# Pooled attention and a two-layer network: k of six batches loaded in blocks of 32 columns and transposed by VectorE, the second batch's q in rows and by TensorE

## The chip, the cores and the metric

The kernel runs on one core of one Trainium2 chip. The metric is the device time of one execution in microseconds (us). A profiled execution has a span, from its first instruction to its last, and an execution time that is a little longer.

## The reference, cut to what matters

q, k and v have shape (8, 8, 576, 64): 8 batches, 8 heads, 576 positions, 64 values. k and v are averaged over groups of eight rows, so each head has 72 keys.

```python
k_p = k.reshape(B, H, Sp, pool, D).mean(axis=3)      # Sp = 72, pool = 8
v_p = v.reshape(B, H, Sp, pool, D).mean(axis=3)
scores = scale * q @ k_p.T ; scores -= max(scores)
attn = exp(scores) / (sum(exp(scores)) + 1e-9)
x = (attn @ v_p).transpose(0, 2, 1, 3).reshape(4608, 512)
h = x @ w_in                                         # 512 x 2048
out = maximum(0.01 * h, h) @ w_out                   # 2048 x 512
```

All is float32. q and k are drawn eight times larger than the usual tenth of a normal draw.

## The kernel before, in words

**The network** takes most of the time. The 4608 rows of x are worked in nine chunks of 512. For each of 16 slices f of the inner size, `m1` (L745) multiplies (ph, four pieces of the model size, L754 to L756), applies the leaky step on ScalarE (L759) and splits the result into a high and a low part (gh L762, gl L763); `m2` (L767) multiplies back into four accumulators (acc, L778 to L780). Each product is three matmuls, high by high, low by high and high by low, in a reduced-precision type; the weights are split in the same way once, early, by `convert` (L169): L184, L185 and L194 on ScalarE, L186, L187, L190 and L195 on VectorE. The chunks go through in "runs" (L738): the first eight slices of chunk 0, all of chunk 1, the other eight of chunk 0, then chunks 2 to 8.

**The attention** of a batch is cut into tiles of 128 positions (and one of 64), the tiles into pieces (`PIECES`, L60), and its steps are put in between the slices of the network. The order of TensorE is written out by hand: for batch 0 in `FIRST`, for batch 1 and 2 by `line_up` (L644), from batch 3 on (`VIA`) by `line_up_via` (L701). The other engines and the queues of DMAs follow the order that the scheduler works out from this. The steps are:

- `load_k` (L265): k of a batch is read as two tiles of 128 partitions (k0 and k1, L241: 64 pooled keys of two heads on each) and one of 64 partitions for the last 8 keys (krem, L251). `pooled` (L226) adds eight rows in three steps (L229, L229, L235), by VectorE for batch 0 and by GpSimd after that. k's last sum is written twice, side by side (copies=2). v is loaded in the same way (L289, with vrem, L259, for its last keys).
- `place_k` (L335): TensorE transposes the sums (pk, four, and pkr for the last keys), ScalarE (L339, L346) and VectorE (L340, L347) scale them into kT, in which the heads of a pair stand in separate halves.
- `load_q` (L316): for batch 0 a tile of q is one DMA in rows; for the others it is 16 DMAs (L332), each of one block of 32 columns of every other row group, in pieces of 128 bytes. `q_unit` (L375) turns a tile: for batch 0 by four TensorE transposes (pq, L385) and a ScalarE copy (L387), for the others by one VectorE transpose of 32 by 32 blocks (L381).
- `s_unit` (L403): scores of four heads (pss, L410), the maximum (red, L418), four exponentials with their sums (e, L420).
- `norm_unit` (L428) divides (L431, L432 on VectorE, `at` L434 and L438 on GpSimd) and TensorE transposes `at` (pp, L500). From batch 3 on `norm_via` (L447; L450, L451, `at` L454 and L460) writes `at` to memory (`rows`, L466) and `fetch_via` (L469) reads it back in 32-column blocks (`blocks`, four DMAs for each, L475), which VectorE transposes (L480).
- `p_unit` (L493) splits that (L502, L503 on ScalarE, L506, L510 on VectorE) and `av_unit` (L514) multiplies by v (pa, L525 to L528). Its result is x of the network.

All loads, and `rows`, `blocks` and the stores of the output, are issued from SyncE's one queue (SPq), in order. The `raw` tiles of a batch's k0, k1, krem, v0, v1 and vrem take turns in two buffers, so krem can be issued only once the sums of k0 are done, and v0 once those of k1 are done. q has two buffers, `at` and `blocks` share three, the tiles with tag `o` (output, weight conversion, transposed `blocks`) three. A batch's k and v are loaded about one run ahead. PSUM gives batch 0 eight banks for its steps; every later batch has two (`bank`, L207).

Of the kernel before, what the change touches and what calls it, by code (L numbers as in the profile page):

```python
# [10 lines left out]
F32 = mybir.dt.float32  # L11
# [4 lines left out]
ALU = mybir.AluOpType  # L16
# [8 lines left out]
def tile_pooled_attention_ffn(  # L25
# [9 lines left out]
    nc = tc.nc  # L35

    P = 128
    B, H, S, D = q.shape
    POOL = 8
    SP = S // POOL  # L40
    MAIN = 64
    REM = SP - MAIN
    DM, DFF = moe_w_in.shape
    NK = DM // P
# [27 lines left out]
    KSCALE = 1.0 / (POOL * 8.0)  # L72
# [3 lines left out]
    one = ctx.enter_context(tc.tile_pool(name="one", bufs=1))  # L76
    two = ctx.enter_context(tc.tile_pool(name="two", bufs=2))
    five = ctx.enter_context(tc.tile_pool(name="outs", bufs=3))
# [15 lines left out]
        out=copies, in_=ident.rearrange("p (h c j) -> p c h j", h=4, c=4), axis=AX.XY, op=ALU.add  # L94
# [6 lines left out]
        out=heads, in_=ident.rearrange("p (h x) -> p h x", h=4), axis=AX.X, op=ALU.add  # L101
# [6 lines left out]
    for g in range(2):  # L108
        r = slice(32 * g, 32 * g + 32)
# [6 lines left out]
    kT = const.tile([P, NK, 2, SP], F32, name="kT")  # L116
# [29 lines left out]
    def spare(f, i, shape, dtype, name):  # L146

        return wts.tile(shape, dtype, tag=f"w{i}_{f}", name=name)
# [58 lines left out]
    def bank(b, name):  # L207
        nonlocal turn
        pool, tag = banks[turn % len(banks)] if b == 0 else banks[0]
        turn += 1  # L210
        return pool.tile([P, NK, P], F32, tag=tag, name=name)
# [8 lines left out]
    def raw_tile(b, nm):  # L220
        shape = [P, 2, POOL * D]
        if (b, nm) in RAW:
            return spare(*RAW[b, nm], shape, F32, f"{nm}raw{b}")
        return two.tile(shape, F32, tag="raw", name=f"{nm}raw{b}")

    def pooled(eng, dst, raw, n, copies=1):  # L226

        for w in (256, 128):
            eng.tensor_tensor(  # L229
                raw[:n, :, 0:w], raw[:n, :, 0:w], raw[:n, :, w : 2 * w], op=ALU.add  # L230
            )
        a, b = raw[:n, :, 0:64], raw[:n, :, 64:128]
        if copies > 1:
            a, b = (x.unsqueeze(2).broadcast_to(dst.shape) for x in (a, b))
        eng.tensor_tensor(dst, a, b, op=ALU.add)  # L235

    def load_main(b, src, g, nm):

        raw = raw_tile(b, f"{nm}{g}")
        for i in range(2):  # L240
            nc.sync.dma_start(  # L241
                raw[64 * i : 64 * i + 64, :, :],
                src[b, 4 * g + i : 4 * g + 4 : 2, : MAIN * POOL, :].rearrange(
                    "p (s a) d -> s p (a d)", a=POOL
                ),
            )
        return raw

    def load_k_rem(b):
        raw = raw_tile(b, "krem")  # L250
        nc.sync.dma_start(  # L251
            raw[:64, 0, :],
            k[b, :, MAIN * POOL :, :].rearrange("h (s a) d -> h s (a d)", a=POOL),
        )
        return raw

    def load_v_rem(b):
# [4 lines left out]
        )  # L262
        return raw

    def load_k(b):  # L265
        sums = one.tile([P, NK, 2, D], F32, tag="ksum", name=f"ksum{b}")
        rem = one.tile([64, 1, 2, D], F32, tag="kremsum", name=f"kremsum{b}")
        eng = nc.vector if b == 0 else nc.gpsimd
        raws = []

        def start():
            raws.extend(load_main(b, k, g, "k") for g in range(2))
            raws.append(load_k_rem(b))

        def finish():
            if b > 1:
                raws.append(load_main(b, k, 0, "k"))
            pooled(eng, sums[:, 0:2], raws[0], P, 2)
            if b > 1:
                raws.append(load_main(b, k, 1, "k"))  # L280
            pooled(eng, sums[:, 2:4], raws[1], P, 2)
            if b > 1:
                raws.append(load_k_rem(b))
            pooled(eng, rem, raws[2][:, 0:1, :], 64, 2)
            return sums, rem

        return start, finish
# [28 lines left out]
    def load_q(b, t):  # L316
        s0, n = tiles[b][t]
        if b == 0:
            qr = one.tile([P, H, D], F32, tag=f"xh1_{t}" if t < NK else "xl1_0", name=f"q{b}_{t}")
        else:  # L320
            qr = two.tile([P, H, D], F32, tag="q", name=f"q{b}_{t}")
        if b == 0:
            nc.sync.dma_start(qr[:n], q[b, :, s0 : s0 + n, :].rearrange("h s d -> s h d"))
            return qr

        blocks = qr.rearrange("a h d -> a (h d)").rearrange("a (p g d) -> a p g d", p=NK, d=32)
        src = q[b, :, s0 : s0 + n, :].rearrange("(p i) (g s) (c d) -> i c s p g d", i=2, s=32, c=2)
        for i in range(2):
            for c in range(2):
                r = 32 * (2 * i + c)  # L330
                for p in range(NK):
                    nc.sync.dma_start(blocks[r : r + 32, p, : n // 32, :], src[i, c, :, p])  # L332
        return qr

    def place_k(b, sums, rem):  # L335
        pk = bank(b, f"pk{b}")
        for p in range(NK):
            nc.tensor.transpose(pk[:, p, :], sums[:, p, :, :].rearrange("s i d -> s (i d)"), ident)
        nc.scalar.mul(kT[0:64, :, 0, 0:MAIN], pk[0:64, :, 0:64], KSCALE)  # L339
        nc.vector.tensor_scalar_mul(kT[64:128, :, 1, 0:MAIN], pk[64:128, :, 64:128], KSCALE)  # L340
        pr = bank(b, f"pkr{b}")
        nc.tensor.transpose(
            pr[:, 0, 0:64], rem.rearrange("s o i d -> s (o i d)"), ident[:64, :64]
        )
        prv = pr[:, 0, 0:64].rearrange("d (p i j) -> d p i j", p=NK, i=2)
        nc.scalar.mul(kT[0:64, :, 0, MAIN:], prv[0:64, :, 0, :], KSCALE)  # L346
        nc.vector.tensor_scalar_mul(kT[64:128, :, 1, MAIN:], prv[64:128, :, 1, :], KSCALE)  # L347
# [26 lines left out]

    def q_unit(b, t, qr):  # L375
        n = tiles[b][t][1]
        if b > 0:

            qT = two.tile([P, NK, P], F32, tag="qT", name=f"qT{b}_{t}")
            blocks = qr.rearrange("a h d -> a (h d)").rearrange("a (p s) -> a p s", p=NK)  # L380
            nc.vector.transpose(qT[:, :, :n], blocks[:, :, :n])  # L381
            return qT
        pq = bank(b, f"pq{b}_{t}")
        for p in range(NK):
            nc.tensor.transpose(pq[:, p, :n], qr[:n, 2 * p : 2 * p + 2, :], ident[:n, :n])  # L385
        qT = two.tile([P, NK, P], F32, tag="qT", name=f"qT{b}_{t}")
        nc.scalar.copy(qT[:, :, :n], pq[:, :, :n])  # L387
        return qT
# [183 lines left out]
    def attention(b):  # L572
# [5 lines left out]
        def loads():  # L578
            (start_k, st["k"]), (start_v, st["v"]) = load_k(b), load_v(b)
            start_k()  # L580
            q_of[b, 0] = load_q(b, 0)
            q_of[b, 1] = load_q(b, 1)
            start_v()
            for t in range(2, 5):
                q_of[b, t] = load_q(b, t)

        def loads1():
            (start_k, st["k"]), (start_v, st["v"]) = load_k(b), load_v(b)
            start_k()
            start_v()  # L590

        def lk():
            st["ks"] = load_k(b)[1]() if b > 1 else st["k"]()
# [4 lines left out]
        def ku():  # L598
            place_k(b, *st["ks"])
# [4 lines left out]
        def qu(t):  # L604
            def f():
                st["qT", t] = q_unit(b, t, q_of[b, t])
                after = every.index((b, t)) + 2
                if after < len(every) and every[after] not in q_of:
                    q_of[every[after]] = load_q(*every[after])
            return f  # L610
# [245 lines left out]
    for b in range(2, B):  # L856
        for j, piece in enumerate(PIECES[b]):
            c = 2 + (2 * TAIL + S * (b - 2) + piece[0][0]) // CH
# [89 lines left out]
```

## Time and profile before

| | |
|---|---|
| time, median of three runs | 984.65 us (981.51 to 985.26) |
| the profiled execution's own time | 983.37 us |
| its span | 981.6 us |
| mean granted TensorE clock | 0.974 |
| TensorE busy | 922.0 us |
| VectorE, ScalarE, GpSimd busy | 410.2, 414.5, 185.4 us |

A row of the profile names a group of instructions, or one, by its line in the kernel, its engine and the names of what it writes and reads. PE is TensorE, DVE VectorE, ACT ScalarE, POOL GpSimd, and SPq the queue of DMAs that SyncE issues. In a timeline a row begins with its start and its length in us, and the bracket at its end tells how long the engine was idle before it and what ended that. In a table by stretches a row holds the span, then busy time and instructions of PE, PE's weight loads, DVE, ACT and POOL, then the granted clock (1.00 is full speed), the busy share of the 16 DMA engines and GB/s.

### The profile page before, as it was taken

What the parts mean: (1) busy time and instruction counts of PE and PEld (TensorE: products, weight loads), DVE (VectorE), ACT (ScalarE), POOL (GpSimd) and SP (SyncE); (2) the same over time, 40 slices, a digit from 0 to 9 for tenths busy, and PEclk for the clock granted to TensorE, in tenths of its full rate; (3) what the DMA queues carried; (4) which work ended last, traced back from release to release, by engine and by line L of the source; (5) the groups of instructions that cost most, each with busy time, mean ns of one, the idle gap of its engine ahead of it and who ended that gap; (6) DMA issues with size and microseconds to landing.
All of it is one profiled execution on the core that took longest, in us unless ns stands there. A gap on an engine that the chain in (4) does not pass through costs nothing. (4 is left out here: it accounts for less than half of the span.)

```text
span 981.6 us, 13210 instructions
## 1 busy us (share of the span) xinstructions
PE 922.0 (94%) x4246; PEld 757.0 (77%) x4246; DVE 410.2 (42%) x987; ACT 414.5 (42%) x1351; POOL 185.4 (19%) x342
## 2 busy tenths in 40 slices
PE   4557989999999998999999999999999999999998
PEld 4446768888887877888888888777878888888886
DVE  5978757513324324334333543354334532321111
ACT  4756766423434333434343444343444433332212
POOL 3610120220106540132112321231111001000000
PEclk8677999999999999999999999999999999999999
DMA  9765332231005432242223332332222110201001
GB/s 249 190 187 158 107 89 67 68 90 46 15 11 145 123 92 50 79 105 61 65 83 87 85 81 79 76 73 65 67 49 63 49 52 25 48 1 44 1 1 43
DMA packets 138469, 75.21 MB, mean 77 GB/s; under 512 B 107552, under 2 KB 121504, under 8 KB 138400
## 3 DMA queue, kind: packets, MB, share of 16 engines
q1 hardware_dynamic: 138400, 74.38, 28.8%
q8 instruction: 33, 0.54, 0.2%
q14 instruction: 36, 0.29, 0.1%
HBM read 54.98 MB, written 19.33 MB: 76 GB/s over the span
## 5 line engine op out<-in xcount | busy, mean ns | idle before, releaser
L754 PE MATMUL ph<-xh,w 128*128 128x512 f32 x576 | 231.2, 401 | 0.0
L778 PE MATMUL acc<-w,gh 128*128 128x512 f32 x576 | 231.0, 401 | 0.0
L756 PE MATMUL ph<-xh,w 128*128 128x512 f32 x576 | 226.6, 393 | 0.0
L755 PE MATMUL ph<-xl,w 128*128 128x512 f32 x576 | 226.6, 393 | 0.0
L779 PE MATMUL acc<-w,gh 128*128 128x512 f32 x576 | 225.8, 392 | 0.0
L780 PE MATMUL acc<-w,gl 128*128 128x512 f32 x576 | 225.7, 392 | 0.0
L763 DVE TENSOR_TENSOR gl<-ph,gh 128x512 fp32r<-128x512 f32 x144 | 98.9, 686 | 242.0 <-ACT gh L762 241.0
L759 ACT ACTIVATE ph<-ph 128x512 f32<-128x512 f32 x144 | 84.1, 584 | 267.2 <-PE ph L756 267.1
L420 ACT ACTIVATE e<-pss,red 128x72 f32<-128x72 f32 (+1 forms) x320 | 98.0, 320 | 92.8 <-DVE red L418 92.3
L756 PEld LDWEIGHTS ph<-xh,w 128*128 128x128 f32 x576 | 109.2, 190 | 23.7
L780 PEld LDWEIGHTS acc<-w,gl 128*128 128x128 f32 x576 | 108.7, 189 | 23.5
L754 PEld LDWEIGHTS ph<-xh,w 128*128 128x128 f32 x576 | 109.0, 189 | 23.1 <-issue 1.6
L778 PEld LDWEIGHTS acc<-w,gh 128*128 128x128 f32 x576 | 108.7, 189 | 22.7 <-issue 1.4
L755 PEld LDWEIGHTS ph<-xl,w 128*128 128x128 f32 x576 | 109.2, 190 | 21.0
L779 PEld LDWEIGHTS acc<-w,gh 128*128 128x128 f32 x576 | 108.8, 189 | 20.7
L454 POOL TENSOR_TENSOR at<-e,red 128x128 f32<-128x128 f32 (+1 forms) x100 | 37.8, 398 | 318.3 <-DVE red L451 216.5
L762 ACT CAST gh<-ph 128x512 fp32r<-128x512 f32 x144 | 84.7, 588 | 3.7
L418 DVE TENSOR_REDUCE red<-pss 128x4 f32<-128x288 f32 (+1 forms) x80 | 36.0, 452 | 82.6 <-PE pss L410 82.5
L420 ACT ACTIVATION_READ_ACCUMULATOR e<-pss,red 128x1 f32 (+1 forms) x320 | 65.7, 205 | 0.0
L502 ACT CAST pT_hi<-pp 128x256 fp32r<-128x256 f32 (+1 forms) x80 | 30.0, 378 | 81.0 <-DVE pp L480 67.3
L410 PEld LDWEIGHTS pss<-kT,qT 128*128 128x128 f32 (+1 forms) x320 | 48.2, 188 | 19.6 <-ACT qT L387 5.0
L410 PE MATMUL pss<-kT,qT 128*128 128x144 f32 (+1 forms) x320 | 55.1, 300 | 8.8 <-ACT qT L387 4.2
(99 smaller groups left out, 818.2 us busy)
## 6 DMA issues: line engine op xcount, KB each, us to landing
out_dram<-o SPq DMA_DIRECT2D x35, 256.0 KB
w_bits<-in_moe_w_in_dram SPq DMA_DIRECT2D x16, 512.0 KB
w_bits<-in_moe_w_out_dram SPq DMA_DIRECT2D x16, 512.0 KB
rows<-at SPq DMA_DIRECT2D x40, 192.0 KB
blocks<-rows SPq DMA_DIRECT2D x160, 48.0 KB
q<-in_q_dram SPq DMA_DIRECT2D x448, 16.0 KB
k0raw<-in_k_dram SPq DMA_DIRECT2D x16, 256.0 KB
k1raw<-in_k_dram SPq DMA_DIRECT2D x16, 256.0 KB
```

The lines of the kernel that those rows point to most:

```text
L410: nc.tensor.matmul(sc[:n, 2 * SP * i : 2 * SP * (i + 1)], qT[:, p, :n], kT[:, p, :, :].rearrange("d i s -> d (i s)"), start=True, stop=True,)
L420: ins = nc.scalar.activation(e[:n, h, :], scv[:n, h, :], AF.Exp, bias=mx[:n, h : h + 1], accum_out=sm[:n, h : h + 1],)
L454: nc.gpsimd.tensor_tensor(at[:n, :, i, :].rearrange("a (h f) j -> a h f j", h=2), e[:n, 2 * i : 2 * i + 2, 0:MAIN].rearrange("a h (f j) -> ...
L754: nc.tensor.matmul(ph, w[:, 0, ks], xh[kk], start=kk == 0, stop=False)
L755: nc.tensor.matmul(ph, w[:, 0, ks], xl[kk], start=False, stop=False)
L756: nc.tensor.matmul(ph, w[:, 1, ks], xh[kk], start=False, stop=kk == NK - 1)
L759: nc.scalar.activation(ph, ph, AF.Prelu, alpha=0.01)
L762: casts.append(nc.scalar.copy(gh, ph))
L763: nc.vector.tensor_tensor(gl, ph, gh.bitcast(F32), op=ALU.subtract)
L778: nc.tensor.matmul(a, gh[:, r], hi, start=first, stop=False)
L779: nc.tensor.matmul(a, gh[:, r], lo, start=False, stop=False)
L780: nc.tensor.matmul(a, gl[:, r], hi, start=False, stop=last)
```

## The change

Two things are changed. For batches 2 to 7, k is read by 8 DMAs into each of the two main tiles and 16 into the tile of the last keys, in pieces of 128 bytes, such that each partition holds one pooled key of one half of a head's 64 columns. GpSimd adds eight rows in three steps (fold) into one tile of sums, not written twice any more. VectorE transposes the sums in blocks of 32 by 32 into a tile kt (tag `o`), and ScalarE and VectorE scale kt into kT. No TensorE transpose of k is left in these batches. For batch 1, a tile of q is read by one DMA in rows and turned by TensorE and ScalarE, as batch 0's is.

```diff
+    def load_k_blocks(b):
+        sums = one.tile([P, NK * SP], F32, tag="ksum", name=f"ksum{b}")
+        main = sums[:, : NK * MAIN].rearrange("a (p k d) -> a p k d", p=NK, k=2)
+        rem = sums[:, NK * MAIN :]
+
+        def fold(raw, out):
+            for w in (4, 2):
+                nc.gpsimd.tensor_tensor(
+                    raw[:, :, 0:w], raw[:, :, 0:w], raw[:, :, w : 2 * w], op=ALU.add
+                )
+            nc.gpsimd.tensor_tensor(out, raw[:, :, 0], raw[:, :, 1], op=ALU.add)
+
+        def finish():
+            for g in range(2):
+                raw = raw_tile(b, f"k{g}")
+                for i in range(2):
+                    for c in range(2):
+                        r = 32 * (2 * i + c)
+                        for p in range(2):
+                            nc.sync.dma_start(
+                                raw[r : r + 32, p, :].rearrange("s (a d) -> s a d", d=32),
+                                k[b, 4 * g + 2 * p + i, : MAIN * POOL, 32 * c : 32 * c + 32].rearrange(
+                                    "(s a) d -> s a d", a=2 * POOL
+                                ),
+                            )
+                fold(...)
+            raw = raw_tile(b, "krem")
+            for i in range(2):
+                for c in range(2):
+                    for p in range(NK):
+                        r = 32 * (2 * i + c) + 8 * p
+                        nc.sync.dma_start(
...
+            fold(raw[:, 0:1, : POOL * 32].rearrange("x o (a d) -> x o a d", d=32), rem.unsqueeze(1))
+            return main, rem
+        return None, finish
+
     def load_k(b):
+        if b > 1:
+            return load_k_blocks(b)
...
     def load_q(b, t):
-        if b == 0:
+        if b < 2:
             nc.sync.dma_start(qr[:n], q[b, :, s0 : s0 + n, :].rearrange("h s d -> s h d"))
             return qr
...
     def place_k(b, sums, rem):
+        if b > 1:
+            t = five.tile([P, NK, SP], F32, tag="o", name=f"kt{b}")
+            nc.vector.transpose(
+                t[:, :, 0:MAIN].rearrange("d p (s k) -> d p k s", k=2), sums
+            )
+            nc.vector.transpose(t[:, :, MAIN:], rem)
+            nc.scalar.mul(kT[0:64, :, 0, :], t[0:64], KSCALE)
+            nc.vector.tensor_scalar_mul(kT[64:128, :, 1, :], t[64:128], KSCALE)
+            return
...
     def q_unit(b, t, qr):
-        if b > 0:
+        if b > 1:
```

**VectorE, between 49 and 62 us.** Before (w_t and w are steps of the weight conversion, qT_0 and qT_1 tiles of batch 1, red_4_0 and red_4_1 the maximum and then the sum of batch 0's last tile; the ISA at L190 is the custom instruction of the conversion):

```order
L190 ISA w_t_534<-w_bits_178,w_t_534 128x1024
L381 STREAM_TRANSPOSE qT_0_771<-q_0_365 128x512
L543 TENSOR_TENSOR xl_3_424<-pa_1_3_561,xh_3_420 128x256
L187 SCALAR_TENSOR_TENSOR w_t_599<-w_bits_180,w_t_599 128x512
L418 TENSOR_REDUCE red_4_0_611<-pss_4_0_607 64x4
L418 TENSOR_REDUCE red_4_1_621<-pss_4_1_617 64x4
L381 STREAM_TRANSPOSE qT_1_838<-q_1_581 128x512
L195 TENSOR_TENSOR w_2_533<-w_t_534,w_2_533 128x512
L190 ISA w_t_599<-w_bits_180,w_t_599 128x1024
L431 TENSOR_SCALAR red_4_0_611<-red_4_0_611 64x4
L432 RECIPROCAL red_4_0_611<-red_4_0_611 64x4
```

Now the same place on VectorE (lines after L265 stand further down in the changed kernel: L605 was L543, L480 was L418, L493 was L431, L494 was L432):

```order
L190 ISA w_t_519<-w_bits_178,w_t_519 128x1024
L605 TENSOR_TENSOR xl_3_409<-pa_1_3_546,xh_3_405 128x256
L187 SCALAR_TENSOR_TENSOR w_t_569<-w_bits_180,w_t_569 128x512
L480 TENSOR_REDUCE red_4_0_581<-pss_4_0_577 64x4
L480 TENSOR_REDUCE red_4_1_591<-pss_4_1_587 64x4
L195 TENSOR_TENSOR w_2_518<-w_t_519,w_2_518 128x512
L190 ISA w_t_569<-w_bits_180,w_t_569 128x1024
L493 TENSOR_SCALAR red_4_0_581<-red_4_0_581 64x4
L494 RECIPROCAL red_4_0_581<-red_4_0_581 64x4
```

The two transposes of batch 1's q are gone, one of which stood ahead of L431; the rest keeps its order.

**SyncE's queue in batch 3, where k and v of batch 4 are loaded.** Before (k0raw, k1raw and kremraw are k of batch 4, rows_0_0 and rows_0_1 the first tile of batch 3):

```order
L241 DMA k0raw_3232<-in_k_dram 64x2x512 x2
L241 DMA k1raw_3238<-in_k_dram 64x2x512 x2
L251 DMA kremraw_3244<-in_k_dram 64x1x512
L466 DMA rows_0_0_3200<-at_0_0_3196 128x384
L241 DMA v0raw_3263<-in_v_dram 64x2x512 x2
L332 DMA q_4_3352<-in_q_dram 32x4x32
L241 DMA v1raw_3269<-in_v_dram 64x2x512 x2
L332 DMA q_4_3352<-in_q_dram 32x4x32 x4
L466 DMA rows_0_1_3293<-at_0_1_3289 128x384
```

Now, on the same queue (L528 was L466, L385 was L332):

```order
L528 DMA rows_0_0_3190<-at_0_0_3186 128x384
L287 DMA k0raw_3221<-in_k_dram 32x16x32 x8
L287 DMA k1raw_3233<-in_k_dram 32x16x32 x8
L302 DMA kremraw_3245<-in_k_dram 8x8x32 x16
L241 DMA v0raw_3279<-in_v_dram 64x2x512 x2
L528 DMA rows_0_1_3309<-at_0_1_3305 128x384
L385 DMA q_4_3368<-in_q_dram 32x4x32
L241 DMA v1raw_3285<-in_v_dram 64x2x512 x2
```

k's five DMAs have become 32 and stand behind the first `rows`; the second `rows` and q_4 follow all of them.

**GpSimd in batch 3.** Now (at_0_0 to at_1_0 are the tiles that `rows` are written from; the sums of k0 stood ahead of at_0_0 before):

```order
L516 TENSOR_TENSOR at_0_0_3186<-e_0_0_3135,red_0_0_3136 128x4x32 x2
L522 TENSOR_TENSOR at_0_0_3186<-e_0_0_3135,red_0_0_3136 128x4x32
L229 TENSOR_TENSOR vremraw_2467<-vremraw_2467 64x128
L235 TENSOR_TENSOR vremsum_2454<-vremraw_2467 64x64
L516 TENSOR_TENSOR at_0_1_3305<-e_0_1_3202,red_0_1_3203 128x4x32 x2
L522 TENSOR_TENSOR at_0_1_3305<-e_0_1_3202,red_0_1_3203 128x4x32
L516 TENSOR_TENSOR at_1_0_3398<-e_1_0_3352,red_1_0_3353 128x4x32 x2
L522 TENSOR_TENSOR at_1_0_3398<-e_1_0_3352,red_1_0_3353 128x4x32
L274 TENSOR_TENSOR k0raw_3221<-k0raw_3221 128x4x128
L274 TENSOR_TENSOR k0raw_3221<-k0raw_3221 128x4x64
L277 TENSOR_TENSOR ksum_3220<-k0raw_3221 128x128
```

Three tiles of `at` now come ahead of k0's sums, on whose buffer krem's DMAs wait.

More of the change, by code (lines that the diff above doesn't have):

```diff
@@ L263, in load_v_rem @@
         return raw
+    def load_k_blocks(b):
[21 more added lines that the diff above has]
+                            )
+                fold(
+                    raw.rearrange("x p (k a d) -> x (p k) a d", k=2, d=32),
+                    main[:, 2 * g : 2 * g + 2].rearrange("x p k d -> x (p k) d"),
+                )
[5 more added lines that the diff above has]
+                        nc.sync.dma_start(
+                            raw[r : r + 8, 0, : POOL * 32].rearrange("s (a d) -> s a d", d=32),
+                            k[b, 2 * p + i, MAIN * POOL :, 32 * c : 32 * c + 32].rearrange(
+                                "(s a) d -> s a d", a=POOL
+                            ),
+                        )
+            fold(
+                raw[:, 0:1, : POOL * 32].rearrange("x o (a d) -> x o a d", d=32),
+                rem.unsqueeze(1),
+            )
+            return main, rem
+        return None, finish
     def load_k(b):
+        if b > 1:
+            return load_k_blocks(b)
         sums = one.tile([P, NK, 2, D], F32, tag="ksum", name=f"ksum{b}")
@@ L335, in place_k @@
     def place_k(b, sums, rem):
+        if b > 1:
+            t = five.tile([P, NK, SP], F32, tag="o", name=f"kt{b}")
+            nc.vector.transpose(
+                t[:, :, 0:MAIN].rearrange("d p (s k) -> d p k s", k=2), sums
+            )
+            nc.vector.transpose(t[:, :, MAIN:], rem)
+            nc.scalar.mul(kT[0:64, :, 0, :], t[0:64], KSCALE)
+            nc.vector.tensor_scalar_mul(kT[64:128, :, 1, :], t[64:128], KSCALE)
+            return
         pk = bank(b, f"pk{b}")
```

## The prediction

> **What bounds the kernel now.** I read the page first: busy time by engine and the chain that ended last.
>
> ```profile
> PE 922.0 (94%) x4246; PEld 757.0 (77%) x4246; DVE 410.2 (42%) x987; ACT 414.5 (42%) x1351; POOL 185.4 (19%) x342
> PE 30%; SPq 1%; DMA 1%; ACT 0%; DVE 0%; issue 0%; POOL 0%; DVEq 0%; POOLq 0%; ACTq 0%
> q1 hardware_dynamic: 138400, 74.38, 28.8%
> ```
>
> TensorE works 922.0 of 981.6 us, and no other engine half of that; the transfers take 28.8% of the 16 DMA engines. Only two things can move the end: less work for TensorE while it is full, or a shorter pause where it is not. So next the busy time by stretch (span, sum, then PE, PEld, DVE, ACT, POOL, granted clock, DMA share, GB/s).
>
> ```profile
> 50.00:75.00 25.00, 13.60 (x56) 10.66 (x57) 17.97 (x42) 14.42 (x42) 3.27 (x4) 0.70 0.65 190
> 75.00:100.00 25.00, 19.98 (x79) 15.67 (x78) 20.39 (x47) 16.15 (x51) 3.36 (x6) 0.82 0.47 144
> 150.00:175.00 25.00, 25.00 (x112) 20.71 (x111) 21.13 (x41) 18.07 (x34) 0.00 (x0) 1.00 0.26 85
> 350.00:375.00 25.00, 21.02 (x93) 16.33 (x92) 10.29 (x26) 10.68 (x43) 8.43 (x16) 0.99 0.42 102
> 60.00:65.00 5.00, 2.08 (x6) 1.58 (x7) 4.90 (x12) 1.00 (x3) 3.27 (x4) 0.50 1.04 364
> 65.00:70.00 5.00, 3.39 (x17) 2.81 (x16) 3.60 (x9) 3.35 (x7) 0.00 (x0) 0.78 0.49 138
> 70.00:75.00 5.00, 4.93 (x18) 4.01 (x17) 3.95 (x10) 4.05 (x10) 0.00 (x0) 0.56 0.62 175
> ```
>
> From 150 us on TensorE is full, and a pause shows as in 350 to 375 us (21.02). The early stretches lose more: 11.4 us are idle between 50 and 75 us and 5.0 in the next 25. I asked for TensorE's pauses in both places (start, length, instruction, idle before it and its releaser).
>
> ```profile
> 62.59 0.47 PE L500 MATMUL pp<-ident,at 64*128 64x64 f32 x2 [8.93 <-POOL at L434]
> 82.90 0.76 PE L410 MATMUL pss<-kT,qT 128*128 128x144 f32 x4 [3.80 <-DVE kT L347]
> ...
> 370.04 0.39 PE L756 MATMUL ph<-xh,w 128*128 128x512 f32 x1
> 374.41 0.63 PE L525 MATMUL pa<-pT_hi,v_hi 128*128 128x320 f32 x1 [3.98 <-ACT pT_hi L502]
> ```
>
> **The early part: batch 1's q.** What the 8.93 us wait for, on VectorE, on SyncE's queue and on GpSimd:
>
> ```profile
> 52.52 0.70 DVE L381 STREAM_TRANSPOSE qT<-q 128x512 f32<-128x512 f32 x1
> 54.05 0.80 DVE L418 TENSOR_REDUCE red<-pss 64x4 f32<-64x288 f32 x2
> 59.33 0.71 DVE L381 STREAM_TRANSPOSE qT<-q 128x512 f32<-128x512 f32 x1 [4.48 <-ACT w_bits L185]
> 61.13 0.15 DVE L431 TENSOR_SCALAR red<-red 64x4 f32<-64x4 f32 x1
> ```
>
> ```profile
> 46.22 0.39 SPq L162 DMA_DIRECT2D w_bits<-in_moe_w_in_dram x1
> 55.25 0.98 SPq L332 DMA_DIRECT2D q<-in_q_dram  x2
> ```
>
> ```profile
> 61.63 0.90 POOL L434 TENSOR_TENSOR at<-e,red 64x256 f32<-64x256 f32 x1 [18.58 <-DVE red L431]
> ```
>
> VectorE runs in order. Its second transpose of batch 1's q waited 4.48 us with the profile naming ScalarE; but the last two of the sixteen pieces of that q were issued at 55.25, so I read the wait as their landing. Queued behind the transpose are two steps of the weight conversion and the L431 that lets GpSimd make `at`. The change takes both transposes off VectorE. Then the exponentials of batch 0's last tile are what L431 still needs; the first four of them end on ScalarE here:
>
> ```profile
> 55.63 0.20 ACT L420 ACTIVATION_READ_ACCUMULATOR e<-pss,red 64x1 f32 x1
> ```
>
> So L431 can start at 55.9 and, with the 0.3 us of L431 and its reciprocal, GpSimd at about 56.1, where it starts at 61.63 now: 5.5 earlier. ScalarE's and VectorE's conversion work has no slack of that size (20.39 of 25 us in the next stretch), so I carry 5.2 of it to 72 us. The 3.80 at 82.90 waits for kT, which VectorE makes between conversion steps; it comes earlier by the same, and by 1.8 more as batch 1's later transposes leave VectorE. Gain: 5.2 + 1.8 = 7.0.
>
> What comes in instead are TensorE transposes and ScalarE copies of the same kind as batch 0's:
>
> ```profile
> L385 PE MATMUL pq<-ident,q 128*128 128x128 f32 x16 | 3.7, 389 | 0.0
> L387 ACT COPY qT<-pq 128x512 f32<-128x512 f32 x4 | 2.5, 612 | 1.1 <-PE pq L385 1.1
> L381 DVE STREAM_TRANSPOSE qT<-q 128x512 f32<-128x512 f32 x28 | 19.7, 702 | 4.7 <-ACT w_bits L185 4.5 <-DMA rows<-at 0.2
> ```
>
> Five tiles of four transposes: the group's 3.7 us for 16 are 0.23 each, so 20 × 0.23 = 4.6 us if all lie on the path at that early clock. The bound from below is the pitch of the k transposes at full clock (next part), 0.64 for five, 0.13 each: 2.6 us; where TensorE pauses anyway they cost nothing. Half of them fall before 90 us, where it pauses, so I take 2.0. The copies are five times 0.61 us of ScalarE in place of five times 0.70 of VectorE; ScalarE stands at 58% to 65% there, and they hide. In all the early part gives 7.0 − 2.0 = 5.0 (bounds: +4.6 when nothing is gained, −12 when the clock gains too).
>
> The clock: after the pause it is granted at 0.50, 0.78 and 0.56 in the three 5-us windows above. "TensorE: Matmul & The Clock Gate" of the Trainium skill (Part 1) says that the clock halves after an idle window of about 3.4 us and comes back after a busy one; the rows agree. By that rule a pause cut to about 3 us may leave the clock up, and the sum would be lower by the gain worked out under the first rival.
>
> **The k of batches 2 to 7, TensorE's side.** In steady state, on the chain that ended last:
>
> ```profile
> 728.65 0.44 PE pk L338 x4
> 729.29 0.43 PE ph L754
> ```
>
> The four transposes and the fifth for the rest take 729.29 − 728.65 = 0.64 us of a full engine. They go for six batches: 6 × 0.64 = 3.8 us, all on the path. VectorE's replacement is a transpose of 256 columns and one of 32 per batch; its nearest row, 0.70 for 512 columns, bounds it from above, about 0.6 for both, on an engine 42% busy with k's sums ready early. Hidden; uncovered it would be 6 × 0.6 = 3.6 us.
>
> **Its side on the queues.** Five DMAs per batch (L241, L251) become 32 in the same queue, SyncE's, where `rows` and `blocks` of the attention stand too. Batch 3 is where TensorE waits on that queue:
>
> ```profile
> 331.78 0.63 SPq L251 DMA_DIRECT2D kremraw<-in_k_dram  x1
> 333.54 0.35 SPq L466 DMA_DIRECT2D rows<-at  x1
> ...
> 341.49 0.63 SPq L466 DMA_DIRECT2D rows<-at  x1
> ...
> 361.45 0.51 SPq L466 DMA_DIRECT2D rows<-at  x1
> 362.00 3.66 SPq L332 DMA_DIRECT2D q<-in_q_dram  x5
> 365.76 1.32 SPq L475 DMA_DIRECT2D blocks<-rows  x3
> 367.18 0.49 SPq L466 DMA_DIRECT2D rows<-at  x1
> 367.72 10.27 SPq L475 DMA_DIRECT2D blocks<-rows  x21
> 378.04 7.54 SPq L332 DMA_DIRECT2D q<-in_q_dram  x16
> ```
>
> ```profile
> 331.01 0.74 POOL L235 TENSOR_TENSOR ksum<-k0raw 128x256 f32<-128x256 f32 x1
> 350.99 0.76 POOL L454 TENSOR_TENSOR at<-e,red 128x128 f32<-128x128 f32 x2 [2.04 <-ACT ph L759]
> ```
>
> ```profile
> 369.91 0.58 DVE L480 STREAM_TRANSPOSE pp<-blocks 128x384 f32<-128x384 f32 x1 [8.27 <-DMA blocks<-rows]
> ```
>
> krem uses the buffer of k0, so its DMA stands in the queue until GpSimd has summed k0: 331.01 + 0.74, issue at 331.78. In the changed order k's 32 DMAs come behind the first `rows`, and GpSimd sums k0 only behind the `at` of 350.99, which I put some 5 us earlier since GpSimd is then free of other work: sums done about 349.5. Then 16 issues of krem; a q issue of 16 takes 7.54 us, 0.47 each, and at 0.43 they end at 356.5. The second `rows` (341.49 before) goes at about 358, the rest of q, v and `rows` follow, and the last `rows` of the piece (367.18) goes at about 372. Fourteen of the next batch's q issues have moved behind the blocks, which saves about 6 us of the queue. The first `blocks` is then complete at 373.4, the last that the pause waits for lands at about 378.6, and L525 starts at about 379.4 where it starts at 374.41: +5.0. From below, −2: the order itself removes ten q issues ahead of the blocks; from above +9, if krem's issues take the 0.63 of L251's row each.
>
> At the later batches the same burst stands 30 to 50 us ahead of the need. I allow +0.7 for all four (−1 to +5).
>
> **Small pieces.** k of a batch comes in 9216 pieces of 128 bytes, not 576 of 2 KB. The queue's mean piece takes 0.288 × 981.6 × 16 / 138400 = 0.033 us of one engine, so six batches add at most 55296 × 0.033 / 16 = 114 us, spread over a span with 0.26 to 0.65 in use: hidden, save in a burst. "DMA: Bandwidth & Descriptors" of the Trainium skill (table of properties, "Min transfer for line-rate") wants at least 512 bytes, which speaks against the change; by it alone the loads would last longer, the case of the last rival. No row above times a single piece.
>
> **Sum.** −5.0 − 3.8 + 5.0 + 0.7 = −3.1. The profiled execution took 983.37 us (span 981.6), within 0.2% of the runs' median of 984.65: 983.37 − 3.1 = 980.3.
>
> **Rivals.** First, the clock stays up early. The three windows lose at most 5 × (0.50 + 0.22 + 0.44) = 5.8 us to the clock; with 4 of them back and only +2.0 at batch 3 the sum is −5.0 − 4.0 − 3.8 + 2.0 = −10.8: 972.6. For it: the pause of 8.93 shrinks to about 3; against it: DMA is full there (1.04) and conversion follows closely.
>
> Second, the queue's burst decides, slower than before: krem's DMA holds SyncE's queue behind GpSimd's sums at every batch, not only at 3. Price: +10 at batch 3 (21 blocks issued after a 372 that becomes 377) and +2.5 at each of four later ones: −5.0 − 3.8 + 20 = +11.2, 994.6. It decides once krem's issue comes over 5 us later than my 349.5; for it, the 8.27 us that VectorE already waits for `blocks`; against it, the page's chain spends only 1% on SPq.
>
> Third, the early gain is taken by the weights: L431 earlier, but conversion (VectorE 20.39 of 25) sets the pace. Then +2.0 − 3.8 + 5.0 + 0.7 = +3.9: 987.3.
>
> Fourth, the small pieces clog the rings: 9216 × 0.033 / 16 = 19 us of full use per batch; if `blocks` of batch 3 queue behind half of it, +9.5 more there: 989.8.
>
> **How the numbers follow.** Half a per cent, 4.9 us, is about what a measurement of this kernel can tell from no change. Chances: forecast 0.43, first 0.25, second 0.13, third 0.13, fourth 0.06. Faster takes the first rival and a third of the forecast, where batch 3 costs nothing: 0.39. Slower takes the second, some of the third and fourth: 0.18. Same: 0.43. The range reaches from 970 (first rival with a covered batch 3) to 990 (third and fourth), and leaves the second out; the forecast's own is 976 to 986.
>
> **What would show it.** Right: the pause at 62.59 shorter by over 5 us, no pk from batch 2 on, the pause at 374.41 longer by some 5 with `rows` late on SyncE's queue. Wrong: a pause as long as before ahead of pp, new pauses before pa in later batches, or pss waiting for kT from VectorE.

## The result, and the profile after

The changed kernel takes 1010.90 us (median, 1010.28 to 1012.12) where the one before takes 983.08 us on the same chip: ratio 1.0279, 95% interval 1.0255 to 1.0302. It is slower by 28 us; 980.3 was forecast, and 990 was the end of the range. The page of the profiled execution first: busy time, the queue's pieces, and the chain that ended last.

```profile
PE 922.5 (91%) x4236; PEld 758.5 (75%) x4236; DVE 413.2 (41%) x988; ACT 418.5 (41%) x1350; POOL 177.2 (18%) x342
q1 hardware_dynamic: 186304, 74.38, 29.8%
PE 68%; SPq 13%; DVE 5%; ACT 4%; DMA 4%; issue 3%; POOL 2%; DVEq 0%; POOLq 0%; ACTq 0%
```

TensorE is busy for 922.5 us, as long as before (922.0), in a span of 1008.7 us instead of 981.6. So the time is in pauses (and in matmuls that are longer after them), and SPq, 1% of the chain before, is 13% of it now. The stretches show where:

```profile
50.00:75.00 25.00, 16.73 (x75) 12.54 (x75) 22.71 (x53) 19.80 (x54) 2.44 (x4) 0.84 0.54 173
75.00:100.00 25.00, 22.95 (x116) 18.62 (x114) 21.45 (x51) 19.62 (x69) 5.87 (x10) 0.94 0.50 150
350.00:375.00 25.00, 13.37 (x60) 10.49 (x58) 3.79 (x8) 4.97 (x15) 11.16 (x21) 0.86 0.37 91
375.00:400.00 25.00, 16.73 (x69) 14.27 (x70) 9.16 (x23) 6.81 (x20) 0.04 (x1) 0.73 0.33 61
550.00:575.00 25.00, 16.51 (x67) 13.45 (x66) 8.02 (x21) 6.74 (x23) 6.04 (x10) 0.80 0.35 81
```

Early TensorE has more work done than before (16.73 and 22.95 us against 13.60 and 19.98); it loses around 375 us and again around 560 us, and a third time around 670. Its pauses:

```profile
57.21 0.72 PE L562 MATMUL pp<-ident,at 64*128 64x64 f32 x3 [2.96 <-POOL at L496]
73.28 0.66 PE L447 MATMUL pq<-ident,q 128*128 128x128 f32 x4 [2.43 <-DVE kT L402]
...
383.27 0.64 PE L587 MATMUL pa<-pT_hi,v_hi 128*128 128x320 f32 x1 [19.90 <-ACT pT_hi L564]
...
563.16 0.63 PE L587 MATMUL pa<-pT_hi,v_hi 128*128 128x320 f32 x1 [8.28 <-ACT pT_hi L564]
675.05 0.64 PE L587 MATMUL pa<-pT_hi,v_hi 128*128 128x320 f32 x1 [8.67 <-ACT pT_hi L564]
```

The first is that of 8.93 us, shorter and earlier. The second stands in place of the 3.80 us: it ends with VectorE's kT of batch 1 too, but what waits is the first of the new transposes of q. The third had 3.98 us and has 19.90. The last two are new: before, the product with v waited at most 1.06 us after batch 3.

I lined up the 576 first matmuls of `m1` (L754 before, L816 after) and took the difference of their starts. By the time in the changed kernel it is −5.5 us at 135 us, −7.1 at 360, +9.7 at 390, +21.4 at 572, +29.2 at 681 and +27.2 at the end. So 16.8 us were lost at batch 3, and 11.7 and 9.5 at the two later pauses; the rest between them is, in sum, a small gain. A pause costs more than its length: in the 4 us from 563 us on the granted clock is 0.50.

```profile
563.00:567.00 4.00, 3.63 (x11) 3.09 (x12) 1.81 (x4) 1.10 (x4) 2.28 (x3) 0.50 0.84 221
```

That agrees with "TensorE: Matmul & The Clock Gate" of the Trainium skill (Part 1): half clock after an idle window.

What SyncE's queue does ahead of the pause at batch 3 (start, length of the group, what is issued):

```profile
336.17 0.38 SPq L528 DMA_DIRECT2D rows<-at  x1
336.59 5.32 SPq L287 DMA_DIRECT2D k0raw<-in_k_dram  x8
342.00 5.27 SPq L287 DMA_DIRECT2D k1raw<-in_k_dram  x8
347.37 11.40 SPq L302 DMA_DIRECT2D kremraw<-in_k_dram  x16
358.88 1.34 SPq L241 DMA_DIRECT2D v0raw<-in_v_dram  x2
360.26 0.59 SPq L528 DMA_DIRECT2D rows<-at  x1
...
375.06 0.50 SPq L528 DMA_DIRECT2D rows<-at  x1
375.61 11.00 SPq L537 DMA_DIRECT2D blocks<-rows  x23
```

Between the first `rows` and the second stand 22 us of k. The 16 DMAs of the last keys take 0.71 us each, from one to the next. The queue does not stand still for GpSimd here: k0's sums are done at 346.40 us, k1's last DMA is issued until 347.27, and the first of the 16 follows at 347.37. GpSimd's `at` of the piece's third tile also comes late, since v0's sums stand ahead of it and v0 is issued behind krem:

```profile
345.94 0.46 POOL L277 TENSOR_TENSOR ksum<-k0raw 128x128 f32<-128x128 f32 x1
...
363.63 1.26 POOL L229 TENSOR_TENSOR v0raw<-v0raw 128x512 f32<-128x512 f32 x1 [2.09 <-DMA v0raw<-in_v_dram]
364.85 0.75 POOL L516 TENSOR_TENSOR at<-e,red 64x128 f32<-64x128 f32 x2
```

At the later pauses the same DMAs stand among the `blocks` themselves. On SyncE, and why they are so late, on GpSimd and VectorE:

```profile
542.51 3.78 SPq L537 DMA_DIRECT2D blocks<-rows  x8
546.33 10.72 SPq L302 DMA_DIRECT2D kremraw<-in_k_dram  x15
557.10 1.36 SPq L241 DMA_DIRECT2D v0raw<-in_v_dram  x2
558.50 2.00 SPq L537 DMA_DIRECT2D blocks<-rows  x4
```

```profile
494.65 2.10 POOL L274 TENSOR_TENSOR k0raw<-k0raw 128x512 f32<-128x512 f32 x2 [18.97 <-DMA k0raw<-in_k_dram]
...
514.06 0.45 POOL L277 TENSOR_TENSOR ksum<-k0raw 128x128 f32<-128x128 f32 x1
```

```profile
513.79 0.17 DVE L394 STREAM_TRANSPOSE kt<-ksum 128x32 f32<-128x32 f32 x1
```

k0 is there at 494, but its last sum goes into the one tile of sums, which VectorE empties only at 513.96. krem uses k0's buffer, so the order of the queue has it behind that. When its turn comes the queue again does not stand still: the sums are done at 514.51, and the fifteen start 0.04 us after the `blocks` ahead of them. Before, krem stood at the same place among the `blocks`, but it was one DMA:

```profile
531.06 3.93 SPq L475 DMA_DIRECT2D blocks<-rows  x7
535.03 0.67 SPq L251 DMA_DIRECT2D kremraw<-in_k_dram  x1
```

### The profile page after: what moved, and what is told of

It reads as the page before. It is cut to its first block, busy times and chain, and to the rows that moved or that the text cites. A ratio compares the mean times of both kernels' runs of the same rounds, so it can differ in the third digit from the quotient of the medians.

```text
span 1008.7 us, 13301 instructions
## 1 busy us (share of the span) xinstructions
PE 922.5 (91%) x4236; PEld 758.5 (75%) x4236; DVE 413.2 (41%) x988; ACT 418.5 (41%) x1350; POOL 177.2 (18%) x342
## 3 DMA queue, kind: packets, MB, share of 16 engines
q1 hardware_dynamic: 186304, 74.38, 29.8%
HBM read 54.98 MB, written 19.33 MB: 74 GB/s over the span
## 4 chain that ended last, share of the span: by engine, by line
PE 68%; SPq 13%; DVE 5%; ACT 4%; DMA 4%; issue 3%; POOL 2%; DVEq 0%; POOLq 0%; ACTq 0%
PE acc L840 10%; PE acc L841 10%; PE acc L842 10%; PE ph L816 10%; PE ph L818 10%; PE ph L817 10%; SPq L302 5%; SPq L385 4%; PE pss L472 3%; ACT e L482 2%; SPq L537 2%; SPq L287 1%; SPq L241 1%; DMA blocks<-rows 1%; PE pp L562 1%
## 5 line engine op out<-in xcount | busy, mean ns | idle before, releaser
L816 PE MATMUL ph<-xh,w 128*128 128x512 f32 x576 | 231.9, 403 | 0.0
L816 PEld LDWEIGHTS ph<-xh,w 128*128 128x128 f32 x576 | 109.5, 190 | 23.0 <-issue 1.6
L480 DVE TENSOR_REDUCE red<-pss 128x4 f32<-128x288 f32 (+1 forms) x80 | 36.2, 454 | 86.6 <-PE pss L472 86.0
L587 PE MATMUL pa<-pT_hi,v_hi 128*128 128x256 f32 (+2 forms) x72 | 24.2, 336 | 41.1 <-ACT pT_hi L564 38.4
```

The source lines that it names most:

```text
L816: nc.tensor.matmul(ph, w[:, 0, ks], xh[kk], start=kk == 0, stop=False)
```

## The experiments

The theory was the queue: k's added issues on SyncE, above all the 96 of the last keys, hold `rows`, v and `blocks`. Its rivals were the pieces of 128 bytes, the waits of krem for GpSimd's sums, and the shift of the early part. Every ratio is to the kernel before on the same chip.

| run | what is changed | us | ratio (95%) |
|---|---|---|---|
| e1_q_only | batch 1's q alone | 977.63 | 0.994 (0.992 to 0.996) |
| e2_k_only | k alone | 1014.21 | 1.030 (1.028 to 1.033) |
| e3_krem4 | last keys by 4 DMAs, same pieces | 975.22 | 0.991 (0.988 to 0.993) |
| e4_krem_row | last keys by one DMA in rows | 971.48 | 0.987 (0.984 to 0.989) |
| e5_rows16 | e1 with the last keys' rows in 16 DMAs | 978.95 | 0.997 (0.995 to 0.999) |
| e6_act | last keys issued by ScalarE | 1012.83 | 1.031 (1.027 to 1.035) |
| e7_pool | last keys issued by GpSimd | 976.87 | 0.995 (0.993 to 0.997) |
| e8_own | last keys in a place of their own | 1000.85 | 1.019 (1.015 to 1.023) |
| e9_main32 | e4 with 32 DMAs for the main tiles | 994.77 | 1.013 (1.011 to 1.015) |
| e10_pool_main | e4, main tiles issued by GpSimd | 1069.38 | 1.089 (1.086 to 1.092) |
| e11_not4 | batch 4's k as before | 997.56 | 1.015 (1.012 to 1.018) |
| e12_rem_first | e4, last keys ahead of the main tiles | 969.14 | 0.987 (0.984 to 0.990) |

**The two parts alone.** e1 is the kernel before with `b == 0` and `b > 0` replaced in `load_q` and `q_unit`:

```diff
-        if b == 0:
+        if b < 2:
...
-        if b > 0:
+        if b > 1:
```

> Only batch 1's q is changed (rows of 256 bytes, TensorE transposes); k is loaded and placed as before. Both theories: the early gain stands alone, 5 to 7 us off the kernel before, about 977, with the pause of 8.9 us before the transposes of batch 0's last tile cut to about 3 us and the later pauses as before. If the early gain is later eaten by a wait that does not depend on k, 982 to 984.

977.63 us: 0.6% gained, as expected.

e2 is the changed kernel with these two lines as they were.

> Only k of batches 2 to 7 is changed; batch 1's q as before. Queue theory (SyncE's 16 issues for the last keys stand ahead of rows, v and blocks): pauses at batch 3 and at two later batches as in the changed kernel; the loss of the early 5 to 7 us is partly taken back because the pause of batch 3 gets shorter by what TensorE comes later, so 1010 to 1017. Rival (the early part's shift itself moved the order and made the pauses): they shrink, 985 to 1000.

1014.21 us, and the pause of batch 3 stays, from the queue again:

```profile
351.83 11.42 SPq L302 DMA_DIRECT2D kremraw<-in_k_dram  x16
```

```profile
388.55 0.63 PE L587 MATMUL pa<-pT_hi,v_hi 128*128 128x320 f32 x1 [20.12 <-ACT pT_hi L564]
```

It is as long as with the early gain (20.12 against 19.90 us) and ends 5.3 us later. So the early gain is carried through the pause; it is not swallowed there, though only 2.2 us of it are left at the end of the two executions. The shift as a cause is out.

**Issues or pieces.** e3 reads as many pieces of 128 bytes in place of the last keys, by 4 DMAs. The rows that it reads are others than the last keys:

```diff
-                    for p in range(NK):
-                        r = 32 * (2 * i + c) + 8 * p
...
+                    r = 32 * (2 * i + c)
+                    nc.sync.dma_start(
+                        raw[r : r + 32, 0, : POOL * 32].rearrange("s (a d) -> s a d", d=32),
+                        k[b, i, S - 32 * POOL :, 32 * c : 32 * c + 32].rearrange("(s a) d -> s a d", a=POOL),
+                    )
```

> The last keys of k are read by 4 DMAs of 32 partitions instead of 16 of 8 (the same number of pieces of 128 bytes; the rows read are not the last keys of each head, so that part of the data is another). Queue theory: 12 issues of 0.71 us go, 8.5 us per batch; the pause of 19.9 us at batch 3 becomes about 11, those of 8.3 and 8.7 us go: 983 to 988. Rival (the pieces of 128 bytes, or GpSimd's sums that come late, hold the loads): nothing of that changes, 1005 to 1011.

975.22 us, below what the theory gave (the reason is found with e8). The four take 2.52 us in place of 11.40, and the pause of batch 3 is 3.64 us:

```profile
336.83 2.52 SPq L301 DMA_DIRECT2D kremraw<-in_k_dram  x4
```

```profile
365.01 0.63 PE L586 MATMUL pa<-pT_hi,v_hi 128*128 128x320 f32 x1 [3.64 <-ACT pT_hi L563]
```

The pieces as such are out: 9216 of them per batch, and a kernel faster than before.

e4 reads the last keys by the old DMA in rows, with old sums and the one TensorE transpose pkr; the main tiles stay in blocks:

```diff
-            raw = raw_tile(b, "krem")
...
+            rem = one.tile([64, 1, 2, D], F32, tag="kremsum", name=f"kremsum{b}")
+            raw = load_k_rem(b)
+            pooled(nc.gpsimd, rem, raw[:, 0:1, :], 64, 2)
```

> The last keys of k by one DMA in rows as before, summed by GpSimd and transposed by one TensorE transpose (0.13 us per batch); the two main tiles in blocks of 32 columns, transposed by VectorE. Queue theory: 15 issues or 10.6 us per batch go: the pause of batch 3 falls to about 9 us, the later ones go: 981 to 986. Rival (small pieces of the main tiles, 8192 of 9216 per batch, hold the loads): 1003 to 1011.

971.48 us, again below the expectation, with 4.00 us at batch 3 and nothing over 0.6 us later. This beats both kernels.

e5 puts 15 more issues into e1, which has no blocks at all (`load_k_rem` with one DMA for 4 partitions of one head).

> As the first of these runs (batch 1's q changed, k in rows of 2 KB, summed and transposed as before), but the last keys of batches 2 to 7 are read by 16 DMAs of 4 partitions in place of one of 64: same bytes, same pieces of 2 KB, TensorE's transposes of k stay. Queue theory (the issues alone, 15 more of about 0.67 us per batch): the pauses come back, 20 to 30 us above that run's 977.6, so 997 to 1008. Rival (it takes the small pieces as well, or the changed order of GpSimd and VectorE): 977 to 984.

978.95 us: by the letter the rival's figure. But the test was weaker than meant. A DMA of 4 partitions is issued in 0.29 us, not 0.67, so the 16 hold the queue for 5.3 to 5.8 us; and this queue has 12 fewer issues for the main tiles. At batch 3 there is no pause at all, where e1 has 3.42 us. At the two later places there are 1.52 and 4.01 us, where e1 has at most 0.56:

```profile
627.99 5.39 SPq L255 DMA_DIRECT2D kremraw<-in_k_dram  x16
```

```profile
644.67 0.64 PE L534 MATMUL pa<-pT_hi,v_hi 128*128 128x320 f32 x1 [4.01 <-ACT pT_hi L511]
```

Taken alone this run is inconclusive between the queue and its rivals. It shows that the price of an issue can't be taken over from another form of DMA.

**Whose queue.** e6 and e7 are the changed kernel with `nc.sync` replaced by `nc.scalar` or `nc.gpsimd` for the 16 DMAs.

> The changed kernel, but the 16 DMAs of the last keys are issued from ScalarE's queue; pieces, buffers and sums as they are. Queue theory: SyncE's queue is rid of 11 us per batch, 972 to 982; ScalarE issues them for 11 us per batch, which could add up to 5 us where exponentials wait behind them. Rival (the pieces, or the number of DMAs as such): 1003 to 1011.

1012.83 us: a miss for both. SyncE is rid of them, but where ScalarE issues 15 in a row, at 0.8 us each, it does nothing else for 12 us, which TensorE feels:

```profile
302.70 12.19 ACTq L302 DMA_DIRECT2D kremraw<-in_k_dram  x15
```

```profile
316.93 0.58 PE L587 MATMUL pa<-pT_hi,v_hi 128*128 128x256 f32 x1 [9.81 <-ACT pT_hi L564]
```

The pause of batch 3 (9.25 us, at 394.45) and the two later ones (5.39 and 4.84 us) are shorter than in the changed kernel, but still there; what makes them here was not taken apart.

> The changed kernel, but the 16 DMAs of the last keys are issued by GpSimd, which sums them too. Queue theory: 972 to 982, if GpSimd's issues are not above 1 us each; at 2 us each they would hold the attention weights that GpSimd also makes, 985 to 1000. Rival (the pieces, or the number of DMAs as such): 1003 to 1011.

976.87 us, as the queue theory said: same pieces, same number of DMAs, same buffers, off SyncE's queue. GpSimd issues them in 9.27 us for 15, the pause of batch 3 falls to 2.63 us, and the two later ones are gone.

```profile
338.67 9.27 POOL L302 DMA_DIRECT2D kremraw<-in_k_dram  x15 [0.41 <-POOL ksum L277]
```

```profile
373.97 0.41 PE L587 MATMUL pa<-pT_hi,v_hi 128*128 128x320 f32 x1 [2.63 <-ACT pT_hi L564]
```

It is not free either: a pause of 4.50 us at 334.95, which the changed kernel does not have, comes while ScalarE works off what had waited for GpSimd's sums of v (it stood idle for 10.99 and 2.76 us before them).

**Waits or issues.** e8 keeps all 32 issues but puts the raw last keys into the tile of the sums, so that they wait for no sums of k0, and v takes turns with k0 and k1 alone.

> The changed kernel with a place of its own for the last keys of k (inside the tile of the sums), so that their 16 DMAs wait for no sums, and v0, v1 and vrem take turns with k0 and k1 alone. All 32 issues stay on SyncE's queue. Queue theory in its plain form (the issues themselves): the pauses stay within 3 us of the changed kernel's, 1000 to 1011. Rival (the queue stands still behind GpSimd's sums, which is what the prediction's second rival was priced by): 985 to 995.

1000.85 us, by the letter still the queue's figure, but the pauses do not stay within 3 us. That of batch 3 falls from 19.90 to 8.02 us, those later stay:

```profile
372.47 0.64 PE L587 MATMUL pa<-pT_hi,v_hi 128*128 128x320 f32 x1 [8.02 <-ACT pT_hi L564]
...
553.69 0.63 PE L587 MATMUL pa<-pT_hi,v_hi 128*128 128x320 f32 x1 [10.65 <-ACT pT_hi L564]
664.24 0.64 PE L587 MATMUL pa<-pT_hi,v_hi 128*128 128x320 f32 x1 [8.34 <-ACT pT_hi L564]
```

That looks like 10 us for waits on GpSimd's sums, but the queue shows another reason. The last keys of batch 3's own k have moved. In the changed kernel their 16 DMAs come at 301.19 us, shortly ahead of batch 3; here they come over 90 us earlier:

```profile
301.19 11.39 SPq L302 DMA_DIRECT2D kremraw<-in_k_dram  x16
```

```profile
196.16 4.99 SPq L302 DMA_DIRECT2D ksum<-in_k_dram  x7
...
203.28 6.40 SPq L302 DMA_DIRECT2D ksum<-in_k_dram  x9
```

So 11.4 us of issues left the queue ahead of batch 3, the first `rows` goes at 324.56 in place of 336.17 us, and the pause is 11.9 us shorter. It is the issues again, and two loads count at batch 3: batch 4's, and batch 3's own some 45 us ahead of it. Between 285 us and the pause SyncE issues k for 22 to 25 us in e4, e11 and e3, with pauses of 4.00, 5.50 and 3.64 us; for 32 us here (8.02); for 41 to 42 us in e9, e2 and the changed kernel (19.33, 20.12 and 19.90). That is also why e3 and e4 came out below what the theory gave: their issues go from both loads. What e8 does not test is the wait at the later places, since its last keys still share the one tile of sums and stand at the same places in the queue.

**Place or total.** e9 splits each of e4's 16 DMAs of the main tiles in two (16 partitions each):

> As the run with the last keys in rows (971.5 us), but the 16 DMAs of the two main tiles are split into 32 of 16 partitions, the same pieces of 128 bytes; by the order most of the 16 added issues stand where the queue loads k0 and k1, ahead of a batch's rows, and only at batch 3 and once after it near the blocks. SyncE then issues for about as long in all as in the changed kernel (about 525 us). If the place in the queue decides (issues that stand between the blocks that TensorE waits for): 974 to 986, with a pause at batch 3 of up to 12 us. If the queue's total decides: 1000 to 1011 with the pauses of the changed kernel.

994.77 us, between the two again, and each half of the question has its own answer. The later pauses are gone although the queue issues for 521 us in all, summed over its DMAs (527 in the changed kernel, 467 in e4): those DMAs stand ahead of the batch's `rows`, not among its `blocks`. There the place decides. At batch 3 they stand in front of `rows`, and the pause is back whole:

```profile
338.84 10.40 SPq L287 DMA_DIRECT2D k0raw<-in_k_dram  x16
349.34 11.11 SPq L287 DMA_DIRECT2D k1raw<-in_k_dram  x16
```

```profile
385.99 0.63 PE L574 MATMUL pa<-pT_hi,v_hi 128*128 128x320 f32 x1 [19.33 <-ACT pT_hi L551]
```

There 22 us of k between two `rows`, and as many of batch 3's own k before them, do what they did in the changed kernel, whichever DMAs make them.

e11 asks whether batch 3 suffers from the load made during it (batch 4's k) or from a queue that comes late (`b > 1 and b != 4` in `load_k` and `place_k`):

> The changed kernel, but k of batch 4 alone, which is loaded during batch 3, is read and placed as before (five DMAs, TensorE transposes). If that load itself makes the pause of 19.9 us at batch 3: the pause falls to 4 to 8 us and the two later ones stay, 990 to 998. If the queue comes late to batch 3 already, from the load of batch 3's k in blocks: the pause stays at 12 us or more, 1002 to 1009.

997.56 us, and the pause of batch 3 is 5.50 us, with 8.82 and 8.41 us later: the load made during batch 3 is worth 14.4 us of the pause. It does not clear the load before it: e8 left this load as it is, took 16 issues from that one, and shortened the pause by 11.9 us.

**Towards a better version.** e10 is e4 with the main tiles' 16 DMAs issued by GpSimd.

> As the run with the last keys in rows (971.5 us), but the 16 DMAs of k's main tiles are issued by GpSimd, so SyncE's queue is rid of about 10 us per batch more. If that queue still holds TensorE at batch 3 (pause of 4.0 us): 966 to 971. If GpSimd's issues, 0.6 us each by the earlier run, hold its sums or the attention weights: 975 to 990.

1069.38 us, the worst, and a miss for both. On GpSimd's queue such a DMA of 512 pieces does not take 0.67 us as on SyncE's but comes every 2.6 us (the first at 174.77, the sixteenth at 213.56). At the next load, from 304.53 to 345.00 us, `at` of a batch stands behind them:

```profile
174.77 0.81 POOL L285 DMA_DIRECT2D k0raw<-in_k_dram  x1 [49.39 <-ACT ph L806]
177.41 0.67 POOL L285 DMA_DIRECT2D k0raw<-in_k_dram  x1 [1.83 <-issue]
```

```profile
346.61 0.72 PE L547 MATMUL pp<-ident,at 64*128 64x64 f32 x3 [30.18 <-POOL at L481]
```

e12 is e4 with the last keys' three lines ahead of the loop over the main tiles.

> As the run with the last keys in rows (971.5 us), but the last keys are read ahead of the main tiles, so that their one DMA no longer waits for the sums of k0 and v0 waits for those of k0 instead of k1. If the 4.0 us of batch 3's pause come from waits in SyncE's queue: 967 to 971. If they come from the issues and the way through memory: 970 to 974.

969.14 us, and the pause of batch 3, 4.00 us in e4, is 0.80:

```profile
363.87 0.42 PE L572 MATMUL pa<-pT_hi,v_hi 128*128 128x320 f32 x1 [0.80 <-ACT pT_hi L549]
```

k's issues take about as long as in e4 (23 and 22 us between 285 us and the pause), so the pause went by the waits, as the first case had it. The times do not tell the two apart: on their own chips e12 and e4 have the same ratio to the kernel before, 0.987; which is better is not settled.

## Why the prediction was wrong

**The early part: right, with some luck in the sum.** −5.0 was forecast; the matmuls stand 5.5 us earlier from 135 us on, and e1 gains 0.6%. The steps are there too. VectorE passes from the maximum straight to the conversion and L493 (L431 before) starts at 56.04 (forecast 55.9), GpSimd at 56.55 (56.1):

```profile
54.11 0.81 DVE L480 TENSOR_REDUCE red<-pss 64x4 f32<-64x288 f32 x2
...
56.04 0.16 DVE L493 TENSOR_SCALAR red<-red 64x4 f32<-64x4 f32 x1
```

The pause is shorter by 6.0 us. Both terms of the −5.0 were too small, however: 7.0 gained and 2.0 lost were forecast, while the matmuls stand 8.9 us earlier at 102 us and 3.4 of that are lost again by 135 us, 2.10 of it in a pause at 111.89 us in front of the last of q's new transposes. The clock did not stay up, as the first rival had it, but it was better: 0.84 in the stretch from 50 to 75 us, 0.70 before.

**k's transposes: right, as far as can be seen.** −3.8 was forecast for four and one per batch. e4, which keeps the one, has a span 4.3 us below e1's (971.2 against 975.5); four per batch alone are 6 × 0.51 = 3.1, and a pause of 1.24 us before e1's pkr at 318.94, which e4 does not have, is in the difference too. VectorE's two transposes take 0.44 and 0.17 us, the 0.6 of the forecast, and from batch 2 on TensorE waits for the new kT once, for 0.12 us.

**The small pieces: right.** The queue's share went from 28.8% to 29.8%, and e3, with every piece, is faster than before. In the trace a piece of 128 bytes took 12.5 ns of a DMA engine on average and one of 2 KB 109 ns, so small ones cost 1.8 times as much per byte, in line with the rule; but the rule of at least 512 bytes, which the prediction cites from "DMA: Bandwidth & Descriptors" of the Trainium skill (Specifications), changed nothing here that could be measured: with every piece the kernel is not slower. So the last rival, the small pieces, is out.

**Batch 3: right in kind, wrong in size.** The failing step is "16 issues of krem; a q issue of 16 takes 7.54 us, 0.47 each, and at 0.43 they end at 356.5". The row to take was the other one in the same fence, L251's 0.63, which I had only for the upper end: the 16 take 11.4 us. The steps can be compared in e2, where TensorE comes to batch 3 without the early gain: krem's issues start at 351.83 (forecast 349.5), end at 363.3 (356.5), the second `rows` goes at 365.09 (358), the last at 380.39 (372), and L587 starts at 388.55 (379.4). Of the 9.1 us, 2.3 come from a queue still busy with k0 and k1 (0.66 each, not looked at), 4.5 from the 16 issues, 2.3 from what follows, v0's sums in front of the third tile's `at` among it. The first 2.3 have a cause that the prediction left out: the 32 issues of batch 3's own k hold the queue from 295.20 to 317.37 us, so the first `rows` goes at 340.66, where it went at 333.54. TensorE comes 2.0 us earlier, k's transposes of two batches being 1.3 of that; so 20 us of pause, not 9.

**The later batches: wrong in kind.** +0.7 was allowed because "the same burst stands 30 to 50 us ahead of the need". It does for k0 and k1, and not for krem: its DMAs stand among the `blocks`, since they come behind k0's sums, and those behind the one tile of sums, which is emptied only at the next batch's turn. Before, krem stood there as well, as one DMA. I read the changed order at batch 3 only. The two pauses cost 11.7 + 9.5 = 21.2 us, and they alone take the result out of the range; so do the 16.8 us of batch 3 in place of 5.0.

The second rival had the queue and the later batches, but not the cause. It had krem hold the queue behind GpSimd's sums, and was to decide once krem's issue came over 5 us later than 349.5. It came at 347.37 (in e2, without the early gain, at 351.83), and the queue did not stand still there: what holds it is the length of the issues. Its price of +11.2 was too low for the same two reasons as the forecast's.

The sum with measured terms, by the matmuls' starts: −7.1 up to batch 3, +16.8, +11.7, +9.5, and −3.7 in between, gives +27.2 in the profiled execution.

## What to carry to other kernels

When a change replaces a few DMAs by many on one queue, take the price of an issue from a row of the nearest form, and read in the new order what stands behind them at every place where they come, and what already fills the queue ahead of it: here 16 issues of 0.7 us among the transfers that TensorE waited for cost more than all that the change gained. A queue that is issued in order is an engine like the others, although the page counts none of it as busy. The cure was small: the main tiles as changed and the last keys in one DMA of rows, and the kernel is 1.3% faster than the one before, whether they are loaded last (e4) or first (e12).

## What the runs showed of the hardware that was not expected

How long an issue takes on SyncE's queue does not go with its pieces: 0.67 us for 64 pieces of 128 bytes on 8 partitions, 0.63 for 512 on 32, 0.61 for 256 on 32, 0.43 for q's 128, 0.65 for 64 of 2 KB, 0.29 for 4 of 2 KB. From one to the next it is about 0.04 us more. What sets it stays open. On GpSimd's queue the time from one to the next did go with them in the two forms that were run: 0.6 us for 64 pieces (e7), about 2.6 us for 512 (e10). On ScalarE's queue the 64 took 0.68 us, and over a row of 15 the engine computed nothing for 12.7 us.
